# Attention and feed-forward kernel: the hand-written order of the first 16 heads becomes priorities, and the first loads leave on two queues

## The chip, the cores and the metric

The kernel runs on one core of a Trainium2 chip. The metric is device time in microseconds (us) of one execution, as the median of three. The core has five engines with queues of their own: PE (matrix products), DVE (vector), ACT (scalar and activation), POOL, and SP, which here only issues transfers. Each works off its queue in order, so an instruction that waits holds up all behind it on that engine. Transfers between the device's memory and the on-chip memory run on 16 DMA engines; SP and ACT can issue them, and a waiting issue on ACT holds up ACT's arithmetic too.

## What is computed

Eight batches of eight heads of attention, 512 local and 32 global rows, in which a local row sees the 32 global keys and a window of its neighbours, and a global row sees all. The result goes through a feed-forward net with a squared ReLU.

```
s_ll = where(|i - j| <= 32, scale * q_l @ k_l.T, -1e9)
out_l = softmax([scale * q_l @ k_g.T, s_ll]) @ [v_g, v_l]
out_g = softmax(scale * q_g @ [k_g, k_l].T) @ [v_g, v_l]
x = rows of [out_g, out_l], 4608 x 512
h = x @ w_in                      # 512 x 2048, given in float64
g = s * relu(h)**2 + b
out = g @ w_out                   # 2048 x 512, given in float64
```

## The kernel before, in words

A "head" j below is one head for half of the local rows; there are 128, and 16 belong to a batch. For each head PE makes the scores (tile `ps_s`), DVE masks them and takes the least negated value (`least`, tiles `sm`, `nm`), ACT takes exponentials with their sums, DVE the inverses, DVE or ACT divides, PE transposes the result (`turned`), ACT copies it (`pt`) and PE multiplies it by the values (`ps_o`). The scores of the global rows go to `ps_g` and are copied by ACT to `sg`. Eight heads fill one tile of 256 tokens, which is split in a high and a low part (`xst`) for products in three passes.

The feed-forward net takes a tile of tokens in eight groups m: `ps_h` (24 products with w_in), then r = relu on ACT, its square on DVE (`r`), a high part g on ACT, a low part on DVE, and 12 products with w_out into `acc`. Group m of the first tile needs the weight pieces k = 2m and 2m+1. `ps_h` has two buffers: group m+2 can start when `r` of group m is done.

The weights arrive as float64 words, 1 MB for each k (two transfers of 512 KB into `wst`), and are turned into a high and a low float32 part on the chip: `word_exponents` (ACT, L159), `word_shift` (DVE, L165), `word_join` (DVE, L169), `word_high` (a cast on ACT, L174), `word_low` (DVE, L178). There are three staging places, and piece k+3 is loaded when `word_low` of piece k is done. Pieces 0 to 3 go through in two halves each.

The first 16 heads, the 16 weight pieces and the first feed-forward groups make up the "front". Heads 0 to 9 run alone (`head_step`), from head 10 on with a feed-forward group each (`both_step`). In this part the code says in which order ACT, DVE, PE and SP do their work: the loop over j in `window_attention_then_ffn` stands in a `manual_schedule` block, and `behind` keeps some splits of heads 16 to 18 in the written order. After it a scheduler places all instructions by priorities and its own estimate of their durations. POOL and ACT's or DVE's later work is always placed so.

The loads of the first heads are issued by SP (`load32`, `v_load32`, `qg_load`), and the first weight piece by ACT. A transfer may be issued only when the one eight before it in issue order, on whichever queue, has landed, since eight completion counters are used in turn.

At the start PE runs 14 products on constants (`keep_busy`, tile `warm`), then four more after each of the first three heads' scores.

Of the kernel before, what the change touches and what calls it, by code (L numbers as in the profile page):

```python
# [22 lines left out]
P = 128  # L23
# [17 lines left out]


NF = 16
AHEAD = 50


LAG = 10
SPLIT_AT = {8 * t + 9: t for t in range(1, 16)}
# [6 lines left out]
BY_HALVES = 4  # L55
LOADS_AT = {1: 1, 3: 2}
EARLY = 1
KEPT = 19
X_ACT = lambda j: LAG <= j < NF
G_AT = (13, 18)  # L60
G_TR = 3
# [5 lines left out]
def f32(ap):  # L67
    return ap.bitcast(F32)
# [3 lines left out]
def window_attention_then_ffn(ctx: ExitStack, tc: tile.TileContext, qd, qg, kw, vw, vg, qz, qgz, vz, w_in, w_out, sv, bv, out):  # L72
# [67 lines left out]
    def weight_load(k):  # L140
        st = ops.tile([P, 2048], I32, tag=SPOTS[k], name=f"wst{k}", bufs=1 + (SPOTS[k] == "kq"))
        staged[k] = st
        sources = (w_in[k], w_out[k * P:(k + 1) * P, :])
        for i in range(2):
            queue = nc.scalar if k == 0 else nc.sync
            queue.dma_start(st[:, 1024 * i:1024 * (i + 1)], sources[i])
# [57 lines left out]
        nc.sync.dma_start(rv, vw[b, hf, h])  # L204
        st_["rv", j] = rv

    def behind(j, done):
        if j < KEPT:
            tc.keep_in_program_order(done)

    def split(j):
        b, hf, h = slot(j)
        rk, rq = st_.pop(("rk", j)), st_.pop(("rq", j))
        p0 = 64 * (h % 2)
        p1 = 64 - p0
        if h % 2 == 0:
            st_["kq", j] = st_["kq", j + 1] = ops.tile([P, 2048], F32R, tag="kq", name=f"kq{j}", bufs=2)
        kq = st_.pop(("kq", j))[:, 1024 * (h % 2):1024 * (h % 2) + 1024]
        ks, qs = kq[:, 0:NK], kq[:, 512:1024].rearrange("p (i q) -> p i q", i=2)
        behind(j, nc.scalar.copy(out=ks[p0:p0 + 64], in_=rk[p0:p0 + 64]))  # L220
        (nc.gpsimd if K_POOL(j) else nc.vector).tensor_sub(out=ks[p1:p1 + 64], in0=rk[p0:p0 + 64], in1=f32(ks[p0:p0 + 64]))
        behind(j, nc.scalar.copy(out=qs[:, 0, :], in_=rq))  # L222
        nc.gpsimd.tensor_sub(out=qs[:, 1, :], in0=rq, in1=f32(qs[:, 0, :]))  # L223
        st_["ks", j], st_["qs", j] = ks, qs

    def v_split(j):
        rv = st_.pop(("rv", j))
        vs = ops.tile([P, 3, 2, D], F32R, tag="vs", name=f"vs{j}", bufs=2)
        rv4 = rv.rearrange("p (c d) -> p c d", d=D)
        behind(j, nc.scalar.copy(out=vs[:, :, 0, :], in_=rv4))  # L230
        nc.gpsimd.tensor_sub(out=vs[:, :, 1, :], in0=rv4, in1=f32(vs[:, :, 0, :]))  # L231
        st_["vs", j] = vs

# [65 lines left out]
    first_q = ops.tile([P, 1280], F32, tag="vsg", name="first_q", bufs=1)  # L299
    first_v = sb.tile([P, 1280], F32, tag="pg", name="first_v", bufs=1)  # L300

    def load32(j):
        b, hf, h = slot(j)
        if h % 2 == 0:
            if j % 4 == 0:
                rk = sb.tile([P, NK], F32, tag="rk", name=f"rk{j}", bufs=2)
            else:
                rk = ops.tile([P, 384], F32, tag="vs", name=f"rk{j}", bufs=2)[:, 0:NK]
            nc.sync.dma_start(rk, kw[b, hf, h // 2])
            st_["rk", j] = st_["rk", j + 1] = rk  # L310
        rq = first_q[:, HALF * (j % 5):HALF * (j % 5 + 1)]
        nc.sync.dma_start(rq, qz[j])
        st_["rq", j] = rq

    def v_load32(j):
        if j >= NF:
            return
        i = j % 5
        rv = first_v[:, 384 * i:384 * i + 384] if i < 3 else sb.tile([P, 6 * D], F32, tag="rv", name=f"rv{j}")
        nc.sync.dma_start(rv, vz[j])  # L320
        st_["rv", j] = rv

# [58 lines left out]
    def pv32(j):  # L381
        pv_products32(j)
        pv_copy32(j)
# [165 lines left out]
    def g_load(b, h):  # L549
        rv = sb.tile([P, 10 * D], F32, tag="rvg", name=f"rvg{b}_{h}", bufs=1)  # L550
        loaded = nc.sync.dma_start(rv, vg[b, h // 2])
        if b == 0:
            tc.keep_in_program_order(loaded)
        vs = ops.tile([P, 2, 5, 2, D], F32R, tag="vsg", name=f"vsg{b}_{h}", bufs=1)
        for i in range(2):
            rv5 = rv[:, 5 * D * i:5 * D * (i + 1)].rearrange("p (c d) -> p c d", d=D)
            copied = nc.scalar.copy(out=vs[:, i, :, 0, :], in_=rv5)  # L557
            if b == 0:
                tc.keep_in_program_order(copied)
            nc.gpsimd.tensor_sub(out=vs[:, i, :, 1, :], in0=rv5, in1=f32(vs[:, i, :, 0, :]))  # L560
        st_["vsg", b, h] = vs
# [33 lines left out]
    def xg_split(t):
        xs = split_tile(f"xs{t % 2}", f"xst{t}", [2, 4, HALF], 1)
# [190 lines left out]
    def first_steps(j):  # L787
        (head_step if j < LAG else both_step)(j)
# [15 lines left out]
    v_load32(2)
    with tc.manual_schedule(engines={mybir.EngineType.Activation, mybir.EngineType.DVE, mybir.EngineType.PE, mybir.EngineType.SP}):
        scores32(0)
        least(0, st_.pop(("ps", 0)))
        scores32(1)
        for j in range(NF):
            if j == 3:  # L810
                nc.sync.dma_start(s_t, sv.partition_broadcast(P))
                nc.sync.dma_start(b_t, bv.partition_broadcast(P))
            if j in LOADS_AT:
                weight_load(LOADS_AT[j])
            if j == 14:
                qg_load(1)
            first_steps(j)
            for fn in extra.pop(j, []):
                fn()
            if j == NF - 1:  # L820
                ffn_relu(j - LAG)
                ffn_square(j - LAG)
                ffn_high(j - LAG)
                ffn_low(j - LAG)
                turned32(j)
                pv32(j)
                x_split(SPLIT_AT.pop(17))
                split(NF)
                qg_split(1)
# [115 lines left out]
```

## Time and profile before

| | us |
|---|---|
| median of 3 runs | 1018.52 |
| lowest and highest | 1017.27, 1020.16 |
| time of the profiled execution | 1017.95 |
| its span, first to last instruction | 1016.1 |
| PE busy | 990.6 |
| DVE busy | 800.1 |
| ACT busy | 693.9 |

The profiled execution lies 1.85 us around its span. "Busy" of PE counts modelled ends of products that overlap, so it overstates how full PE is where little is to be done. The granted TensorE clock was 1.000, that is, the upper of its two levels.

### The profile page before, as it was taken

How to read it: one execution, taken by the hardware profiler on the slowest of the kernel's cores; microseconds unless marked ns; L12 is line 12 of the kernel's file. 1: busy time of each engine (PE TensorE's matmuls, PEld its weight loads, DVE VectorE, ACT ScalarE, POOL GpSimd, SP SyncE). 2: the span in 40 equal slices, each digit the busy share in tenths (PEclk: the TensorE clock that was granted, in tenths of full speed). 3: DMA queues.
4: the chain of work that ended last, by engine and by line, in shares of the span. 5: the costliest groups of instructions: out<-in, count | busy, mean ns of one | idle time of the engine just before them, and what ended most of it. 6: DMA issues, size and time to landing. Idle time of an engine off the chain costs nothing.

```text
span 1016.1 us, 19944 instructions
## 1 busy us (share of the span) xinstructions
PE 990.6 (97%) x6914; PEld 902.4 (89%) x6914; DVE 800.1 (79%) x2054; ACT 693.9 (68%) x1784; POOL 287.2 (28%) x366
## 2 busy tenths in 40 slices
PE   8798999999999999999999999999999999999998
PEld 5687998989989999999999999999999999999887
DVE  5898778988789788988799788988789788964322
ACT  6998768767677667867678667867678666843222
POOL 1000424424243223424244223424244223401000
PEclk9999999999999999999999999999999999999999
DMA  8873322313132122312132122312132122101000
GB/s 278 304 266 135 95 65 69 91 43 95 31 106 67 49 60 65 91 48 85 45 104 66 44 67 65 91 48 86 44 105 60 49 68 65 61 1 49 23 22 21
DMA packets 63844, 82.03 MB, mean 81 GB/s; under 512 B 7680, under 2 KB 51200, under 8 KB 63744
## 3 DMA queue, kind: packets, MB, share of 16 engines
q1 hardware_dynamic: 63168, 79.46, 25.8%
q10 hardware_dynamic: 576, 1.31, 0.4%
q8 instruction: 54, 0.88, 0.4%
q14 instruction: 46, 0.38, 0.1%
HBM read 71.30 MB, written 9.44 MB: 79 GB/s over the span
## 4 chain that ended last, share of the span: by engine, by line
PE 88%; DVE 5%; ACT 3%; DMA 2%; issue 1%; SPq 0%; DVEq 0%; ACTq 0%
PE acc L664 35%; PE ps_h L620 34%; PE ps_s L441 5%; PE ps_o L469 4%; PE turned L361 2%; PE turned L363 2%; PE ps_og L568 2%; PE ps_g L448 1%; PE turned L542 1%; DMA wst<-in_w_in 1%; PE warm L106 1%; ACT wst L159 1%; DMA wst<-in_w_out 1%; DVE sm L272 1%; DVE sm L242 0%
## 5 line engine op out<-in xcount | busy, mean ns | idle before, releaser
L620 PE MATMUL ps_h<-xst,w_all 128*128 128x256 f32 x3264 | 436.6, 281 | 4.4 <-DVE r L640 1.9
L664 PE MATMUL acc<-w_all,g 128*128 128x512 f32 x1632 | 421.0, 396 | 0.0
L620 PEld LDWEIGHTS ps_h<-xst,w_all 128*128 128x128 f32 x3264 | 408.6, 189 | 12.9 <-DVE r L640 2.1
L664 PEld LDWEIGHTS acc<-w_all,g 128*128 128x128 f32 x1632 | 289.9, 188 | 50.1
L231 POOL TENSOR_TENSOR vs<-rv,vs 128x192 fp32r<-128x192 f32 x112 | 71.4, 638 | 299.9 <-ACT vs L230 287.4
L252 ACT ACTIVATE sm<-sm,nm 128x224 f32<-128x224 f32 x256 | 121.6, 478 | 34.0 <-DVE nm L242 32.9
L640 DVE SCALAR_TENSOR_TENSOR r<-ps_h,s_t,r 128x512 f32<-128x512 f32 x136 | 101.5, 746 | 54.1 <-ACT r L636 52.3
L648 DVE SCALAR_TENSOR_TENSOR g<-r,b_t,g 128x512 fp32r<-128x512 f32 x136 | 110.6, 813 | 39.3 <-ACT g L644 35.2
L644 ACT ACTIVATE g<-r,b_t 128x512 fp32r<-128x512 f32 x136 | 98.5, 725 | 62.1 <-DVE r L640 61.8
L223 POOL TENSOR_TENSOR kq<-rq,kq 128x256 fp32r<-128x256 f32 x112 | 90.0, 804 | 141.6 <-ACT kq L222 129.5
L636 ACT ACTIVATE r<-ps_h 128x512 f32<-128x512 f32 x136 | 81.3, 598 | 69.8 <-PE ps_h L620 61.8
L560 POOL TENSOR_TENSOR vsg<-rvg,vsg 128x320 fp32r<-128x320 f32 x64 | 57.5, 919 | 190.8 <-ACT vsg L557 190.7
L272 DVE TENSOR_SCALAR sm<-sm,nm 128x224 f32<-128x224 f32 x234 | 87.2, 413 | 3.7
L441 PE MATMUL ps_s<-kq 128*128 128x224 f32 x448 | 72.8, 275 | 1.8 <-DVE nm L242 1.8
L441 PEld LDWEIGHTS ps_s<-kq 128*128 128x128 f32 x448 | 66.6, 190 | 8.2 <-POOL kq L223 1.4
L458 ACT CAST pt<-turned 128x416 fp32r<-128x416 f32 x112 | 57.4, 512 | 21.2 <-PE turned L363 20.5
L459 DVE TENSOR_TENSOR pt<-turned,pt 128x416 fp32r<-128x416 f32 x112 | 65.5, 585 | 7.2 <-ACT pt L458 6.5
L452 ACT COPY tg<-ps_g 32x256 f32<-32x256 f32 (+1 forms) x112 | 42.1, 376 | 36.9 <-PE ps_g L448 34.9
L361 PE MATMUL turned<-ident,sm 128*96 128x128 f32 (+1 forms) x256 | 63.3, 273 | 3.8 <-DVE sm L272 2.6
L453 DVE TENSOR_TENSOR sg<-ps_g,tg 32x256 f32<-32x256 f32 (+1 forms) x112 | 48.2, 431 | 21.4 <-ACT tg L452 14.8
L469 PE MATMUL ps_o<-pt,vs 128*128 128x256 f32 x336 | 63.0, 295 | 0.3 <-DVE pt L459 0.3
L363 PE MATMUL turned<-ident,sm 128*128 128x128 f32 x256 | 62.8, 272 | 0.0
(85 smaller groups left out, 1249.7 us busy)
## 6 DMA issues: line engine op xcount, KB each, us to landing
rq<-in_qd SPq DMA_DIRECT2D x112, 128.0 KB, 2.2
rk<-in_kw SPq DMA_DIRECT2D x64, 176.0 KB, 2.3
rv<-in_vw SPq DMA_DIRECT2D x112, 96.0 KB, 1.9
rvg<-in_vg SPq DMA_DIRECT2D x32, 320.0 KB, 3.0
out<-o SPq DMA_DIRECT2D x32, 256.0 KB, 2.3
wst<-in_w_in SPq DMA_DIRECT2D x15, 512.0 KB, 3.9
wst<-in_w_out SPq DMA_DIRECT2D x15, 512.0 KB, 5.4
first_q<-in_qz SPq DMA_DIRECT2D x16, 128.0 KB, 4.9
```

The costliest lines, as they stand in the source:

```text
L223: nc.gpsimd.tensor_sub(out=qs[:, 1, :], in0=rq, in1=f32(qs[:, 0, :]))
L252: nc.scalar.activation(out=p, in_=p, func=AF.Exp, bias=nm[:, 0, blk:blk + 1], scale=-1.0, accum_out=nm[:, 1, blk:blk + 1],)
L272: nc.vector.tensor_scalar(out=p, in0=p, scalar1=ss[:, blk:blk + 1], scalar2=1.0, op0=ALU.mult, op1=ALU.mult,)
L361: nc.tensor.transpose(out=p_t[0:n, s0:s0 + P], in_=sm[:, c0:c0 + n], identity=ident)
L363: nc.tensor.transpose(out=p_t[:, o0:o0 + P], in_=sm[:, c0:c0 + P], identity=ident)
L441: nc.tensor.matmul(p_s[:, W * blk:W * blk + W], lhsT=qs[:, a, blk * P:(blk + 1) * P], rhs=ks[:, KEYS[blk]], start=(a == 0), stop=(a == 1),)
L469: nc.tensor.matmul(p_o[:, :, q], lhsT=vs[0:n, c], rhs=pt[0:n, :, o], start=(c == 0), stop=(c == 1))
L620: nc.tensor.matmul(p_h[:, k], lhsT=wi[:, a, f, c], rhs=xs[:, e, c, :], start=(n == 0), stop=(n == 11),)
L640: nc.vector.scalar_tensor_tensor(out=r, in0=p_h, scalar=s_t, in1=r, op0=ALU.mult, op1=ALU.mult)
L644: nc.scalar.activation(out=g[:, 0], in_=st_["r", m], func=AF.Identity, bias=b_t)
L648: nc.vector.scalar_tensor_tensor(out=g[:, 1], in0=st_.pop(("r", m)), scalar=b_t, in1=f32(g[:, 0]), op0=ALU.add, op1=ALU.subtract,)
L664: nc.tensor.matmul(oacc[t][i], lhsT=g[:, a, k, i * P:(i + 1) * P], rhs=wo[:, e, f, :], start=(pr == 0 and n == 0), stop=(pr == 7 and n == 5),)
```

## The change

The block that fixed the order in the front is gone. The same code in the same sequence now gives priorities, and the scheduler places the instructions on all engines; `behind` and the three other marks that kept program order are gone as well. The loads of the first heads are written in another order and on two queues: the queries of heads 0 and 2, the global queries and the values of head 1 are issued by ACT, the rest by SP, and the first weight piece comes behind the keys and queries of heads 0 to 2 on ACT's queue. The constant AHEAD was not used.

```
-    def load32(j):
+    def load32(j, queue=nc.sync):
...
-        nc.sync.dma_start(rq, qz[j])
+        queue.dma_start(rq, qz[j])
...
-        behind(j, nc.scalar.copy(out=ks[p0:p0 + 64], in_=rk[p0:p0 + 64]))
+        nc.scalar.copy(out=ks[p0:p0 + 64], in_=rk[p0:p0 + 64])
...
     with tc.high_priority(offset=300):
-        load32(0)
+        load32(0, nc.scalar)
         load32(1)
-        qg_load(0)
-        load32(2)
+        qg_load(0, nc.scalar)
+        load32(2, nc.scalar)
         v_load32(0)
+        weight_load(0)
         load32(3)
-        v_load32(1)
-    load32(4)
-    weight_load(0)
-    v_load32(2)
-    with tc.manual_schedule(engines={mybir.EngineType.Activation, mybir.EngineType.DVE, mybir.EngineType.PE, mybir.EngineType.SP}):
-        scores32(0)
-        least(0, st_.pop(("ps", 0)))
-        scores32(1)
-        for j in range(NF):
...
+        v_load32(1, nc.scalar)
+        load32(4)
+        v_load32(2)
+    scores32(0)
+    least(0, st_.pop(("ps", 0)))
+    scores32(1)
+    for j in range(NF):
...
```

What this does to the queues is seen at three places. In the rows the digits behind a name are the head, the group or the piece (`sm1` is head 1, `r4` group 4, `wst13` piece 13), and the last number is the scheduler's own. Lines of the changed kernel are 2 to 9 lower (L174 becomes L172, L640 becomes L632).

ACT at its start, before:

```order
L146 DMA wst0_150<-in_w_in 128x1024
L131 ACT_TABLE_LOAD
L131 ACTIVATE unread_131<-warm_92 128x1
L146 DMA wst0_150<-in_w_out 128x1024
L252 ACTIVATE sm0_165,nm0_166<-sm0_165,nm0_166 128x224 x2
L350 COPY sg0_159<-ps_g1_177 64x256
L270 ACTIVATE sm0_165<-sm0_165,nm0_166 128x224
L252 ACTIVATE sm1_185,nm1_186<-sm1_185,nm1_186 128x224 x2
L377 COPY pt0_224<-turned_83 128x416
L159 ACTIVATE wst0_150<-wst0_150 128x512
L270 ACTIVATE sm1_185<-sm1_185,nm1_186 128x224
L252 ACTIVATE sm2_215,nm2_216<-sm2_215,nm2_216 128x224 x2
```

ACT at its start, now, from its fifth load down to the exponentials of head 2:

```order
L144 DMA wst0_145<-in_w_out 128x1024
L314 DMA first_v_134<-in_vz 128x384
L129 ACT_TABLE_LOAD
...
L157 ACTIVATE wst0_145<-wst0_145 128x512
L344 COPY sg0_157<-ps_g1_175 64x256
L246 ACTIVATE sm0_163,nm0_164<-sm0_163,nm0_164 128x224 x2
L172 CAST w_all_60<-wst0_145 128x512
...
L264 ACTIVATE sm0_163<-sm0_163,nm0_164 128x224
L344 COPY sg0_157<-ps_g3_220 64x256
L246 ACTIVATE sm1_183,nm1_184<-sm1_183,nm1_184 128x224 x2
...
L371 COPY pt0_222<-turned_83 128x416
L246 ACTIVATE sm2_213,nm2_214<-sm2_213,nm2_214 128x224 x2
```

Four loads (queries of head 0, global queries, queries of head 2, the w_in half of piece 0) stand ahead of these rows. Among the rows left out are the exponents of the second half of piece 0 and its cast. So both halves of piece 0 pass through ACT between the first three heads, and the table load has moved behind six loads, of which the fifth and the sixth wait for a landing (the queries of head 0, and the global queries).

DVE at the end of the front, from group 4's square to group 5's, before:

```order
L640 SCALAR_TENSOR_TENSOR r4_934<-ps_h4_867,s_t_90,r4_934 128x512
L258 TENSOR_SCALAR nm15_864<-nm15_864 128x2
L165 TENSOR_SCALAR wst14_851<-wst14_851 128x1024
L262 RECIPROCAL nm15_864<-nm15_864 128x2
L648 SCALAR_TENSOR_TENSOR g4_958<-r4_934,b_t_91,g4_958 128x512
L169 SCALAR_TENSOR_TENSOR wst14_851<-wst14_851 128x1024
L178 TENSOR_TENSOR w_all_60<-wst14_851,w_all_60 128x1024
L165 TENSOR_SCALAR wst15_897<-wst15_897 128x1024
L169 SCALAR_TENSOR_TENSOR wst15_897<-wst15_897 128x1024
L178 TENSOR_TENSOR w_all_60<-wst15_897,w_all_60 128x1024
L640 SCALAR_TENSOR_TENSOR r5_1002<-ps_h5_938,s_t_90,r5_1002 128x512
```

The same stretch now:

```order
L632 SCALAR_TENSOR_TENSOR r4_932<-ps_h4_865,s_t_90,r4_932 128x512
L167 SCALAR_TENSOR_TENSOR wst13_811<-wst13_811 128x1024
...
L176 TENSOR_TENSOR w_all_60<-wst13_811,w_all_60 128x1024
L167 SCALAR_TENSOR_TENSOR wst14_849<-wst14_849 128x1024
L640 SCALAR_TENSOR_TENSOR g4_956<-r4_932,b_t_91,g4_956 128x512
L176 TENSOR_TENSOR w_all_60<-wst14_849,w_all_60 128x1024
L163 TENSOR_SCALAR wst15_895<-wst15_895 128x1024
L167 SCALAR_TENSOR_TENSOR wst15_895<-wst15_895 128x1024
L215 TENSOR_TENSOR kq16_1016<-rk16_675,kq16_1016 64x352
L632 SCALAR_TENSOR_TENSOR r5_1000<-ps_h5_936,s_t_90,r5_1000 128x512
```

The join and the low part of piece 13 have moved from ahead of group 4's square to behind it, the low part of piece 15 behind group 5's, and the split of head 16's keys ahead of that.

PE over the same stretch, before:

```order
L620 MATMUL ps_h5_938<-xst0_294,w_all_60 128x256 x12
L620 MATMUL ps_h6_1065<-xst0_294,w_all_60 128x256 x19
L394 MATMUL ps_o15_953<-pt14_951,rv14_551 128x128 x2
...
L620 MATMUL ps_h5_938<-xst0_294,w_all_60 128x256 x12
...
L664 MATMUL acc0_0_655<-w_all_60,g4_958 128x512 x6
L664 MATMUL acc0_1_656<-w_all_60,g4_958 128x512 x6
L620 MATMUL ps_h6_1065<-xst0_294,w_all_60 128x256 x5
L620 MATMUL ps_h7_1147<-xst0_294,w_all_60 128x256 x24
```

And now:

```order
L612 MATMUL ps_h5_936<-xst0_292,w_all_60 128x256 x16
L612 MATMUL ps_h6_1062<-xst0_292,w_all_60 128x256
L656 MATMUL acc0_0_653<-w_all_60,g4_956 128x512 x2
...
L612 MATMUL ps_h6_1062<-xst0_292,w_all_60 128x256 x15
L388 MATMUL ps_o15_951<-pt14_949,rv14_549 128x128 x2
...
L612 MATMUL ps_h6_1062<-xst0_292,w_all_60 128x256 x8
L435 MATMUL ps_s16_1034<-kq16_1016 128x224
L442 MATMUL ps_g16_1039<-kq16_1016,qgs1_1021 64x256
L435 MATMUL ps_s16_1034<-kq16_1016 128x224 x3
L612 MATMUL ps_h7_1144<-xst0_292,w_all_60 128x256 x8
```

All 24 products of group 5 now stand ahead of group 6's first, which waits for `r4`; 12 of them stood behind it. The scores of head 16 stand ahead of group 7's products, which wait for `r5`.

Names apart, the two orders are the same on PE from its product 2,310 of 6,828 on, and on ACT and DVE from a like place.

## Rows read from the trace of the kernel before

**Rows 1.** Busy time by stretch: from:to, length, engines, PEclk, DMA share, GB/s.
```profile
0.00:20.00 20.00, 17.84 (x80) 10.51 (x80) 8.64 (x37) 10.92 (x31) 3.19 (x15) 1.00 0.81 260
20.00:40.00 20.00, 15.72 (x92) 11.60 (x90) 17.82 (x64) 19.35 (x56) 0.00 (x0) 1.00 0.96 345
40.00:88.00 48.00, 39.85 (x262) 35.04 (x262) 44.39 (x85) 43.21 (x81) 0.00 (x0) 1.00 0.78 266
88.00:300.00 212.00, 206.82 (x1477) 190.76 (x1477) 174.50 (x450) 151.78 (x400) 75.54 (x93) 1.00 0.24 70
300.00:940.00 640.00, 640.00 (x4556) 591.56 (x4555) 532.34 (x1389) 448.52 (x1186) 206.72 (x257) 1.00 0.22 64
```

**Rows 2.** Start of the timeline: start, length, engine, line, operation, idle before and releaser.
```profile
1.19 1.28 ACT L131 ACT_TABLE_LOAD   x1 [1.19 <-PEq L933]
1.46 5.34 PE L106 MATMUL warm<-warm 128*128 128x512 bf16 x14 [1.46 <-DVE warm L101]
5.05 0.33 SPq L320 DMA_DIRECT2D first_v<-in_vz  x1
6.63 0.92 PE L328 MATMUL ps_s<-rk,first_q 128*128 128x224 f32 x4
8.15 0.48 ACT L252 ACTIVATE sm<-sm,nm 128x224 f32<-128x224 f32 x1 [5.46 <-DVE nm L242]
10.98 0.36 ACT L350 COPY sg<-ps_g 64x256 f32<-64x256 f32 x1 [1.79 <-PE ps_g L340]
13.23 0.51 ACT L377 COPY pt<-turned 128x416 f32<-128x416 f32 x1 [0.57 <-PE turned L363]
13.63 0.67 ACT L159 ACTIVATE wst<-wst 128x512 f32<-128x512 f32 x1
...
14.57 0.47 ACT L252 ACTIVATE sm<-sm,nm 128x224 f32<-128x224 f32 x1
15.41 0.19 ACT L252 ACTIVATION_READ_ACCUMULATOR sm<-sm,nm 128x1 f32 x1
```

**Rows 3.** Who waited for whom from 8 to 88 us: total, times, longest.
```profile
ACT w_all L174 <- DVE wst L165: 3.5, 4, 1.2
```

**Rows 4.** Groups by form, front (first three) and 88 to 350 us: busy, mean ns.
```profile
L174 ACT CAST w_all<-wst 128x1024 fp32r<-128x1024 f32 x11 | 12.7, 1157 | 3.5 <-DVE wst L165 3.5
L174 ACT CAST w_all<-wst 128x512 fp32r<-128x512 f32 x8 | 5.4, 670 | 0.0
L169 DVE SCALAR_TENSOR_TENSOR wst<-wst 128x1024 int32<-128x1024 int32 x11 | 13.5, 1223 | 0.1
...
L220 ACT CAST kq<-rk 64x352 fp32r<-64x352 f32 x38 | 18.3, 482 | 0.5
L222 ACT CAST kq<-rq 128x256 fp32r<-128x256 f32 x38 | 15.3, 404 | 1.4 <-DMA rq<-in_qd 1.0
L221 DVE TENSOR_TENSOR kq<-rk,kq 64x352 fp32r<-64x352 f32 x19 | 14.9, 782 | 0.6
```

**Rows 5.** First global queries' transfer (KB, us to landing); weight halves' landing times, all.
```profile
rqg<-in_qgz SPq DMA_DIRECT2D x1, 128.0 KB, 5.2
...
DMA to landing us min/median/max: 3.5/4.6/8.6
```

**Rows 6.** Timeline, scores of head 11 and the end of the front.
```profile
38.46 1.02 PE L328 MATMUL ps_s<-rk,first_q 128*128 128x224 f32 x4
...
86.98 0.74 DVE L640 SCALAR_TENSOR_TENSOR r<-ps_h,s_t,r 128x512 f32<-128x512 f32 x1
87.78 2.45 PE L620 MATMUL ps_h<-xst,w_all 128*128 128x256 f32 x19 [1.88 <-DVE r L640]
93.45 0.63 ACT L636 ACTIVATE r<-ps_h 128x512 f32<-128x512 f32 x1
94.86 0.75 DVE L640 SCALAR_TENSOR_TENSOR r<-ps_h,s_t,r 128x512 f32<-128x512 f32 x1
95.39 3.58 PE L620 MATMUL ps_h<-xst,w_all 128*128 128x256 f32 x29
```

More of the change, by code (lines that the diff above doesn't have):

```diff
@@ L43 @@
 NF = 16
-AHEAD = 50
 LAG = 10
@@ L57 @@
 EARLY = 1
-KEPT = 19
 X_ACT = lambda j: LAG <= j < NF
@@ L205, in v_load @@
         st_["rv", j] = rv
-    def behind(j, done):
-        if j < KEPT:
-            tc.keep_in_program_order(done)
     def split(j):
@@ L219, in split @@
         ks, qs = kq[:, 0:NK], kq[:, 512:1024].rearrange("p (i q) -> p i q", i=2)
-        behind(j, nc.scalar.copy(out=ks[p0:p0 + 64], in_=rk[p0:p0 + 64]))
+        nc.scalar.copy(out=ks[p0:p0 + 64], in_=rk[p0:p0 + 64])
         (nc.gpsimd if K_POOL(j) else nc.vector).tensor_sub(out=ks[p1:p1 + 64], in0=rk[p0:p0 + 64], in1=f32(ks[p0:p0 + 64]))
-        behind(j, nc.scalar.copy(out=qs[:, 0, :], in_=rq))
+        nc.scalar.copy(out=qs[:, 0, :], in_=rq)
         nc.gpsimd.tensor_sub(out=qs[:, 1, :], in0=rq, in1=f32(qs[:, 0, :]))
@@ L229, in v_split @@
         rv4 = rv.rearrange("p (c d) -> p c d", d=D)
-        behind(j, nc.scalar.copy(out=vs[:, :, 0, :], in_=rv4))
+        nc.scalar.copy(out=vs[:, :, 0, :], in_=rv4)
         nc.gpsimd.tensor_sub(out=vs[:, :, 1, :], in0=rv4, in1=f32(vs[:, :, 0, :]))
@@ L311, in load32, with v_load32 @@
         rq = first_q[:, HALF * (j % 5):HALF * (j % 5 + 1)]
-        nc.sync.dma_start(rq, qz[j])
+        queue.dma_start(rq, qz[j])
         st_["rq", j] = rq
-    def v_load32(j):
+    def v_load32(j, queue=nc.sync):
         if j >= NF:
@@ L319, in v_load32 @@
         rv = first_v[:, 384 * i:384 * i + 384] if i < 3 else sb.tile([P, 6 * D], F32, tag="rv", name=f"rv{j}")
-        nc.sync.dma_start(rv, vz[j])
+        queue.dma_start(rv, vz[j])
         st_["rv", j] = rv
@@ L415, in pv_copy32, with qg_load @@
             nc.vector.tensor_copy(out=x_out, in_=p_o)
-    def qg_load(b):
+    def qg_load(b, queue=nc.sync):
         rqg = sb.tile([P, H * SG], F32, tag="xr", name=f"rqg{b}", bufs=1)
-        nc.sync.dma_start(rqg, qgz[0] if b == 0 else qg[b])
+        queue.dma_start(rqg, qgz[0] if b == 0 else qg[b])
         st_["rqg", b] = rqg
@@ L551, in g_load @@
         loaded = nc.sync.dma_start(rv, vg[b, h // 2])
-        if b == 0:
-            tc.keep_in_program_order(loaded)
         vs = ops.tile([P, 2, 5, 2, D], F32R, tag="vsg", name=f"vsg{b}_{h}", bufs=1)
@@ L587, in x_split @@
                 v = slice(2 * i, 2 * i + 2)
-                behind(8 * t + 8, nc.scalar.copy(out=xs_[t][:, 0, v, :], in_=xcur[t][:, v, :]))
+                nc.scalar.copy(out=xs_[t][:, 0, v, :], in_=xcur[t][:, v, :])
         if only != 0:
@@ L592, in x_split @@
                 v = slice(2 * i, 2 * i + 2)
-                behind(8 * t + 8, nc.vector.tensor_sub(out=xs[:, 1, v, :], in0=x[:, v, :], in1=f32(xs[:, 0, v, :])))
+                nc.vector.tensor_sub(out=xs[:, 1, v, :], in0=x[:, v, :], in1=f32(xs[:, 0, v, :]))
     def xg_split(t):
@@ L794, in window_attention_then_ffn @@
     with tc.high_priority(offset=300):
-        load32(0)
+        load32(0, nc.scalar)
         load32(1)
-        qg_load(0)
-        load32(2)
+        qg_load(0, nc.scalar)
+        load32(2, nc.scalar)
         v_load32(0)
+        weight_load(0)
         load32(3)
-        v_load32(1)
-    load32(4)
-    weight_load(0)
-    v_load32(2)
-    with tc.manual_schedule(engines={mybir.EngineType.Activation, mybir.EngineType.DVE, mybir.EngineType.PE, mybir.EngineType.SP}):
-        scores32(0)
-        least(0, st_.pop(("ps", 0)))
-        scores32(1)
-        for j in range(NF):
[L810 to L829, printed above, removed]
+        v_load32(1, nc.scalar)
[5 more added lines that the diff above has]
+    for j in range(NF):
+        if j == 3:
+            nc.sync.dma_start(s_t, sv.partition_broadcast(P))
+            nc.sync.dma_start(b_t, bv.partition_broadcast(P))
+        if j in LOADS_AT:
+            weight_load(LOADS_AT[j])
+        if j == 14:
+            qg_load(1)
+        first_steps(j)
+        for fn in extra.pop(j, []):
+            fn()
+        if j == NF - 1:
+            ffn_relu(j - LAG)
+            ffn_square(j - LAG)
+            ffn_high(j - LAG)
+            ffn_low(j - LAG)
+            turned32(j)
+            pv32(j)
+            x_split(SPLIT_AT.pop(17))
+            split(NF)
+            qg_split(1)
     assert not to_join and not staged and not g_at
```

## The prediction

> **What bounds the kernel now.** I read busy time by stretch first. From 88 us on PE is full: 206.8 of 212 us, then 640 of 640 [rows 1]. From about a third of PE's work on, the two orders are the same, so the change can alter the time in two ways only: by how early PE becomes full, and by the 5.2 us that it stands still between 88 and 300 us. A microsecond saved in the front is then one saved at the end.
>
> In the front PE is not the limit. From 20 to 40 us ACT works 19.35 of 20 us and the transfers take 0.96 of the DMA engines; from 40 to 88 us DVE works 44.4 and ACT 43.2 of 48 us [rows 1]. What may be gained there is the idle time of these two, some 4 us each, and what the start leaves. The timeline shows the start: ACT has nothing to do until 8.15 us, waits 1.79 us more before 10.98, and touches the first weights only at 13.63 [rows 2]. Later ACT's longest wait is that of its cast of the high part, 3.5 us in four cases, for DVE's shift, the instruction just ahead in the same chain [rows 3]. Last I read the end of the front: PE's products of group 6 stand 1.88 us for `r` of group 4 until 87.78; group 7's follow at 95.97 (95.39 and five products of 0.12 us), right behind `r` of group 5, which ends at 95.61 [rows 6]. There PE catches up with ACT and DVE for the last time.
>
> **The change part by part.** *Keys and queries earlier, on two queues.* The first scores follow the 14 warm-up products without a gap (1.46 and 5.34 give 6.80; the first scores' record begins at 6.63) [rows 2], and these products stay. So earlier keys are worth nothing at the first head. Without that cover they would be worth at most one landing, 5.2 us for a load of this size [rows 5].
>
> The Trainium skill, in "DMA: Bandwidth & Descriptors", section "Issuing engines are not separate DMA queues", says that the transfers of all issuers share the same 16 DMA engines and that a second issuer saves only issue time. By it the three loads of queries that leave SP would give at most 1.2 us, at 0.4 us each; by the warm-up's row it is 0. The trace agrees in so far as almost all loads from 20 to 40 us are SP's, and they take 0.96 of the engines.
>
> The price lies on ACT. It has six issues ahead of its table load, and the fifth and sixth wait for landings of the first loads. In the old run the ninth transfer, which waits for the first one's landing, left at 5.05 us [rows 2]; the global queries took 5.2 us to land [rows 5], so after an issue at 1.2 they would let the sixth go at 6.4. With issues of 0.3 to 0.4, the table load of 1.28 [rows 2] and a small activation of 0.2 us, ACT is free between 6.9 and 8.4 us. I take 7.4. The exponents of the first half (0.67) and the copy of global scores (0.36) then put the first exponentials at 8.4 rather than 8.15 [rows 2].
>
> *The first three heads.* From 8.4 the new order has on ACT: exponentials of heads 0, 1 and 2, each a pair with its sum reads, 1.03 us a head (14.57 to 15.60 [rows 2]); two casts of 0.67 [rows 4]; the second exponents of 0.67, one division of 0.47, taken as an exponential's, a copy of 0.36 and a `pt` copy of 0.51 [rows 2]. That is 6.4 us, so head 2's exponentials could be done at 14.8. Before they are done at 15.60 (15.41 and 0.19). At that point the new order has two casts, one half of exponents and one copy more behind it and one division less: 1.34 + 0.67 + 0.36 - 0.47 = 1.9 us. The lead is 0.8 + 1.9 = 2.7 us if nothing waits, 1.7 if ACT is free only at 8.4. DVE has the join and the low part of the same halves between the heads, and PE's next scores wait for DVE, so I take 2.0.
>
> *Heads 3 to 10.* ACT has 0.65 us of idle time left in 20 us and the DMA engines 0.04 of theirs [rows 1], so nothing is gained here, and a lead can be lost. Summed along the issue order, the new one has 10.7 MB out by the keys of heads 14 and 15, among them 0.59 MB that the old one left for later (queries of heads 16 and 17, global values). It wants these keys, for `ps_g15`, ahead of the scores of head 11, which began at 38.46 [rows 6]. The old run had moved 5.2 MB by 20 and 12.1 MB by 40 us; at 345 GB/s it stood at 10.7 MB at 35.9 [rows 1]. The margin is 2.6 us, a little more than the lead, so I keep the lead.
>
> *Heads 10 to 15.* The new order puts other work between a shift and its cast. Of the 3.5 us of these waits [rows 3] I take 1.0 as gained, between 0 (DVE is 92% busy, so ACT then waits elsewhere) and 2.4 us. With the start this is R = 3.0 us, between 1.7 and 5.1.
>
> *The end of the front.* For `r` of group 4 DVE has a join and a low part less ahead (1.22 us each [rows 4]), so group 6 can start 2.4 us earlier and R on top, with 12 products more behind it. But most of this is given back. Ahead of `r` of group 5 ACT has one cast less (1.16) and more: two casts of keys (0.48) and two of queries (0.40) [rows 4], one of global queries and one of values (about 0.4 each, taken as the queries'), net 1.4 us. Its `r` ended at 94.08 and DVE took it at 94.86 [rows 6]; now ACT ends at 94.08 + 1.4 - 3.0 = 92.5. DVE has a low part less and a split of keys more (1.22 against 0.78 [rows 4]), so it is free at 91.4, and `r` is done at 93.2. Group 7 thus starts 2.8 us earlier than 95.97, and PE has the four score products of head 16 behind it, 0.6 us at five times a 0.12 us product. PE gains 3.4 us. Between the two gates it stands still for some 3.5 us: the old stretch of 8.2 us, less 12 products, plus these scores, is 7.4, and the gates lie 11 us apart. For group 8 ACT's splits add 5.3 us, of which R takes 3.0; the other 2.3 lie beside group 7's 24 products (2.8 us) and the output products behind them.
>
> *From 88 to 350 us.* The scheduler placed this part before and does so now, from another state. The 5.2 us of waits [rows 1] may shrink or grow; I take no change, and 2 us either way.
>
> *The other edits.* Where the unmarked splits went is counted above. The constant AHEAD costs nothing, since no instruction used it.
>
> The sum: 1017.95 for the profiled execution, less 3.4, is 1014.5. That execution lies 0.6 us under the median of the three runs, so I say **1014.8 us**, between the two.
>
> **The rivals.** *No net gain.* The front is a reshuffle: ACT and DVE are 90 to 97% busy, and what the start gains is waited out at their next crossing. For it: the idle time from 20 to 88 us is made of waits of about 1 us or less [rows 3]. Against it: the idle time at the start is of another kind, for there was nothing to do. R is then 1.0, group 7 gains 0.8 us, and the time is 1017.5 by the median.
>
> *A larger gain.* R is 5.1 and the later waits halve: 1017.95 - 5.5 - 2.6, about 1010. For it: DVE is what PE waits for at the end, and it loses 2.4 us of work ahead of that place. Against it: two engines over 90% busy and in order rarely pack closer.
>
> *Late keys, slower.* The place is `ps_g15` on PE, ahead of head 11's scores: PE's queue stands until the keys of heads 14 and 15 land, and ACT and DVE have at most one head in stock. SP issues these keys behind two half loads of weights that wait for DVE. Weight halves took 4.6 us to land in the median and 8.6 at most [rows 5]; keys 4.0 us late use up the margin of 2.6, and earlier loads pass the same stretch. If the lead is lost and 3.6 us with it, the time is 1021.6. It decides when these keys land after 38.5 us. For it: 0.96 of the DMA engines busy, and 0.59 MB (1.7 us at 345 GB/s) brought forward into that stretch. Against it: from 40 to 88 us the share is only 0.78 [rows 1], so the queue recovers.
>
> **How the numbers follow.** A difference under 0.3% (3.1 us) is about what a measurement of this kernel can't tell from none. I give 0.40 to the forecast, with its own range of 1013 to 1016.5, of which 0.30 lies below 1015.4; 0.15 to the larger gain; 0.25 to no net gain; 0.20 to late keys. So faster is 0.45 (0.30 and 0.15), same 0.35 (0.10 and 0.25), and slower 0.20. The range goes from 1009.5, just under the larger gain's time, to 1021.0; beyond it lie most of late keys and a few hundredths below.
>
> **What would show it.** On ACT the first exponents at 7 to 8 us, the first exponentials at 8.3 to 9, and head 2's done before 15.3. PE's group 6 starting at 82 to 84 us, group 7 at 92 to 94 behind a wait for `r` of about 3 us, and no wait at `ps_g15`. ACT's waits for the shift well under 3.5 us. PE full from group 7 on, with 3 to 7 us of waits up to 350 us. The forecast fails if PE waits for a load between 20 and 40 us, if group 7 starts later than 95, or if the waits behind it grow by more than 3 us.

## The result, and the profile after

The changed kernel takes **1005.92 us** (1004.15 to 1006.82) against 1019.34 for the kernel before: a ratio of 0.9867, with a 95% interval of 0.9841 to 0.9893. That is 13.4 us faster; the prediction had 1014.8, with a range from 1009.5 to 1021.0, so the result lies 3.6 us below its lower end. The direction was right and the size was not. The profiled execution took 1005.12 us, its span 1003.3. The ratios, here and below, leave out three executions that took far longer than the others of their kernel (1992.87 us of E2, 1098.31 of E5 and 1227.64 of the kernel before).

Busy time by stretch in the changed kernel, with the columns and stretches of [rows 1]:

```profile
0.00:20.00 20.00, 17.57 (x76) 9.69 (x77) 11.25 (x42) 12.68 (x35) 3.19 (x15) 1.00 0.79 272
20.00:40.00 20.00, 16.02 (x94) 12.37 (x92) 18.36 (x65) 19.89 (x55) 0.00 (x0) 1.00 1.04 389
40.00:88.00 48.00, 46.13 (x311) 43.13 (x310) 45.07 (x88) 45.76 (x89) 3.20 (x3) 0.96 0.72 243
88.00:300.00 212.00, 211.44 (x1513) 195.31 (x1512) 182.14 (x475) 155.51 (x414) 80.42 (x95) 1.00 0.26 74
300.00:940.00 640.00, 640.00 (x4562) 591.81 (x4561) 526.18 (x1364) 443.21 (x1168) 204.72 (x254) 1.00 0.22 62
```

Two things are to be seen. PE's idle time before 88 us (length less the first busy number) fell from 14.6 to 8.3 us, most of it between 40 and 88 us: 1.9 us against 8.2. And from 88 to 300 us it fell from 5.2 to 0.6. Together that is 10.9 us. PE's busy time over the whole span fell by 1.7 (990.6 to 988.9), so 12.6 of the span's 12.8 us are accounted for. From 300 to 940 us PE is full in both.

The same view in finer steps shows from when on PE is full:

```profile
40.00:46.00 6.00, 4.13 (x29) 3.52 (x28) 5.58 (x16) 5.95 (x13) 0.00 (x0) 1.00 1.01 379
46.00:50.00 4.00, 4.00 (x21) 4.00 (x22) 3.72 (x10) 4.00 (x8) 0.00 (x0) 0.57 0.86 287
50.00:88.00 38.00, 38.00 (x264) 35.61 (x263) 35.78 (x64) 35.81 (x70) 3.20 (x3) 1.00 0.66 217
```

It is full from 46 us, not from 88. Four rows of its timeline and the two squares `r` that the prediction spoke of show how:

```profile
21.29 0.96 PE L612 MATMUL ps_h<-xst,w_all 128*128 128x256 f32 x3
...
78.32 0.74 DVE L632 SCALAR_TENSOR_TENSOR r<-ps_h,s_t,r 128x512 f32<-128x512 f32 x1
81.25 2.12 PE L612 MATMUL ps_h<-xst,w_all 128*128 128x256 f32 x17
...
89.45 0.75 DVE L632 SCALAR_TENSOR_TENSOR r<-ps_h,s_t,r 128x512 f32<-128x512 f32 x1
...
90.76 0.59 PE L435 MATMUL ps_s<-kq 128*128 128x224 f32 x3 [0.56 <-POOL kq L217]
91.19 1.10 PE L612 MATMUL ps_h<-xst,w_all 128*128 128x256 f32 x8
```

The first feed-forward products run at 21.29 us, in ones to fours between the heads, where the old order had them in blocks of twelve from 41.81 on. The square of group 4 ends at 79.06, that of group 5 at 90.20, 8.7 and 5.4 us earlier than in [rows 6]. PE waits for neither: the last of the 17 products at 81.25 is group 6's first, 4 us after its gate opened, and group 7 follows at 91.19. PE's one wait between 88 and 300 us is the 0.56 us before 90.76, for the split of head 16's keys on POOL.

ACT's waits from 8 to 88 us (the view of [rows 3]) have changed their kind:

```profile
ACT wst L157 <- DMA wst<-in_w_in: 2.4, 1, 2.4
ACT wst L157 <- DMA wst<-in_w_out: 1.6, 3, 0.9
ACT r L628 <- PE ps_h L612: 0.6, 1, 0.6
```

The 3.5 us behind DVE's shift are gone whole; what is left are mostly waits for weights to land.

### The profile page after: what moved, and what is told of

The parts are those of the page before. It is cut to its first block, busy times and chain, and to the rows that moved or that the text cites. A ratio compares the mean times of both kernels' runs of the same rounds, so it can differ in the third digit from the quotient of the medians.

```text
span 1003.3 us, 19931 instructions
## 1 busy us (share of the span) xinstructions
PE 988.9 (99%) x6914; PEld 903.6 (90%) x6914; DVE 800.9 (80%) x2054; ACT 693.5 (69%) x1784; POOL 291.5 (29%) x366
## 4 chain that ended last, share of the span: by engine, by line
PE 90%; DMA 4%; ACT 3%; DVE 1%; issue 1%; SPq 0%; POOL 0%; ACTq 0%; POOLq 0%
PE acc L656 36%; PE ps_h L612 36%; PE ps_s L435 5%; PE ps_o L463 4%; PE turned L355 2%; PE turned L357 2%; PE ps_og L560 2%; DMA wst<-in_w_out 2%; PE ps_g L442 1%; PE turned L536 1%; DMA rk<-in_kw 1%; ACT wst L157 1%; ACT w_all L172 1%; DMA first_q<-in_qz 1%; DMA b_t<-in_bv 1%
## 5 line engine op out<-in xcount | busy, mean ns | idle before, releaser
L632 DVE SCALAR_TENSOR_TENSOR r<-ps_h,s_t,r 128x512 f32<-128x512 f32 x136 | 101.5, 746 | 54.6 <-ACT r L628 52.7
L640 DVE SCALAR_TENSOR_TENSOR g<-r,b_t,g 128x512 fp32r<-128x512 f32 x136 | 111.7, 822 | 36.0 <-ACT g L636 31.6
L217 POOL TENSOR_TENSOR kq<-rq,kq 128x256 fp32r<-128x256 f32 x112 | 93.1, 832 | 138.2 <-ACT kq L216 122.2
L266 DVE TENSOR_SCALAR sm<-sm,nm 128x224 f32<-128x224 f32 x234 | 84.3, 400 | 4.1
```

The source lines that it names most:

```text
L266: nc.vector.tensor_scalar(out=p, in0=p, scalar1=ss[:, blk:blk + 1], scalar2=1.0, op0=ALU.mult, op1=ALU.mult,)
L640: nc.vector.scalar_tensor_tensor(out=g[:, 1], in0=st_.pop(("r", m)), scalar=b_t, in1=f32(g[:, 0]), op0=ALU.add, op1=ALU.subtract,)
```

## Experiments

The theory after the result (A): the gain has two separate causes. ACT, DVE and PE pack closer in the first 100 us, and the attention of the later heads runs ahead of the feed-forward groups when the weights are done, so that PE no longer waits for it between 100 and 300 us. Rivals are named in each expectation. All results stand in one table. "Idle" is the length of the stretch less PE's busy time; "lead" is how long before DVE's square of group 9 the first exponential of head 18 starts on ACT; "clock" is the mean granted clock of the span. Each ratio is taken against the kernel before on the same chip at the same time. Idle time, lead and clock are those of one execution of each kernel.

| kernel | median us | ratio (95%) | idle 0-100 | idle 100-300 | lead | clock |
|---|---|---|---|---|---|---|
| before | 1018.1 to 1019.7 | 1 | 14.6 | 5.2 | 1.1 | 1.000 |
| the change | 1005.9 | 0.9867 (0.9841-0.9893) | 8.8 | 0.0 | 8.2 | 0.998 |
| E1 loads alone | 1019.5 | 1.0007 (0.9996-1.0017) | 14.5 | 5.4 | 1.1 | 0.998 |
| E2 free order alone | 1003.6 | 0.9853 (0.9838-0.9867) | 7.9 | 0.8 | 8.0 | 1.000 |
| E3 marks off | 1019.2 | 1.0009 (0.9997-1.0021) | 12.6 | 3.6 | -0.1 | 0.991 |
| E4 free from head 10 | 1015.3 | 0.9962 (0.9947-0.9976) | 8.7 | 3.2 | 6.4 | 0.995 |
| E5 free to head 9 | 1020.3 | 1.0013 (1.0001-1.0025) | 13.4 | 3.5 | 2.4 | 0.991 |
| E6 ACT, DVE free | 1009.7 | 0.9922 (0.9908-0.9935) | 11.8 | 0.5 | 8.0 | 0.998 |
| E7 PE, SP free | 1023.0 | 1.0055 (1.0036-1.0074) | 14.3 | 6.3 | -0.1 | 0.994 |
| E8 heads 18, 19 late | 1019.4 | 1.0015 (1.0006-1.0024) | 8.4 | 9.8 | -13.1 | 0.992 |
| E9 weights first | 1013.1 | 0.9945 (0.9931-0.9958) | 10.2 | 4.1 | 2.4 | 0.996 |
| E10 one queue | 1003.6 | 0.9851 (0.9838-0.9865) | 8.2 | 0.5 | 8.0 | 1.000 |
| E11 heads to 31 early | 1004.4 | 0.9854 (0.9841-0.9868) | 8.6 | 0.0 | 7.3 | 1.000 |
| E12 heads 18, 19 less late | 1011.0 | 0.9920 (0.9906-0.9933) | 8.3 | 4.9 | 0.2 | 0.998 |
| E13 written, lag 12 | 1025.6 | 1.0061 (1.0047-1.0075) | 23.0 | 0.0 | 15.5 | 0.990 |
| E14 free, lag 12 | 1012.2 | 0.9928 (0.9912-0.9945) | 8.1 | 1.8 | 5.4 | 0.999 |

**E1 and E2: the two halves of the change.** E1 is the kernel before with the new loads, E2 the changed kernel with the old ones.

```
     with tc.high_priority(offset=300):
-        load32(0)
+        load32(0, nc.scalar)
         load32(1)
-        qg_load(0)
-        load32(2)
+        qg_load(0, nc.scalar)
+        load32(2, nc.scalar)
         v_load32(0)
+        weight_load(0)
...
```

> The written order and its marks stay; only the first loads are issued in the new order and on two queues. Theory A: the gain of 13 us has two causes, both from the free order: PE stands idle 8.3 us before 88 us instead of 14.6, and its waits of 5.2 us between 150 and 300 us are gone. The loads give next to nothing, since the warm-up products cover them: 1017 to 1020 us, 3 to 6 us of PE waits between 88 and 300 us. Rival B: earlier keys, queries and values give the head start that all the rest inherits: 1008 to 1013 us.

> The scheduler places the first 16 heads, and the first loads leave in the old order, nearly all on SP. Theory A: nearly the whole gain, 1005 to 1009 us, with PE idle about 8 us before 88 us and under 1 us of PE waits from 88 to 300 us. Rival B: most of the gain is lost with the loads, 1013 to 1018 us.

Busy time from 0 to 100 and 100 to 300 us, of E1:

```profile
0.00:100.00 100.00, 85.55 (x505) 68.33 (x506) 79.64 (x195) 80.73 (x176) 3.19 (x15) 0.98 0.72 250
100.00:300.00 200.00, 194.64 (x1386) 179.11 (x1386) 163.59 (x435) 142.75 (x385) 74.92 (x92) 1.00 0.24 73
```

and of E2:

```profile
0.00:100.00 100.00, 92.12 (x573) 76.68 (x574) 88.11 (x213) 89.70 (x204) 16.09 (x26) 1.00 0.75 264
100.00:300.00 200.00, 199.22 (x1426) 183.87 (x1425) 169.95 (x458) 145.85 (x391) 70.75 (x87) 1.00 0.24 71
```

Theory B falls. E2 is even 1.4 us faster than theory A allowed, though its waits from 88 to 300 us are 2.3 us and not under 1. The loads are worth nothing in the written order, and the free order has the whole gain without them: all three engines do 7 to 9 us more work in the first 100 us than in E1. E2's span is 1.6 us below the changed kernel's at the same idle time (8.7 against 8.8 us); the difference is in PE's busy time (987.3 against 988.9), and the changed kernel has the stretch from 46 to 50 us at a granted clock of 0.57, E2 none below 1.00 before its end.

**E3, E6 and E7: which engines must be free.** Old loads, no marks; the block stands around the same code with all four engines (E3), PE and SP (E6), or ACT and DVE (E7).

```
...
-    for j in range(NF):
...
+    with tc.manual_schedule(engines={mybir.EngineType.PE, mybir.EngineType.SP}):
...
+        for j in range(NF):
...
```

> The written order of the first 16 heads stays and the loads leave as before; only the marks that keep splits of heads 16 to 18, the splits of the first tiles and the first global values in the written order are gone. Theory A: the front is unchanged and the attention of heads 16 to 19 stays late (exponentials of head 16 at about 109 us), so the PE waits from 150 to 300 us stay: 1016 to 1020 us, 4 to 6 us of waits from 88 to 300 us. Rival D: it is the marks that held the later attention back; without them those waits go: 1011 to 1015 us.

> Old loads, no marks; PE and SP keep the written order for the first 16 heads, ACT and DVE are placed by the scheduler. Theory A: before 88 us ACT and DVE are over 90% busy and PE only follows, so their free order gives most of the gain: 1005 to 1010 us, PE idle 8 to 10 us before 88 us. Rival E: what gains is PE's free order, which puts feed-forward products into PE's waits, gets the squares of the groups out earlier and so the heads of the free placement: 1013 to 1019 us, PE idle 12 to 15 us.

> Old loads, no marks; ACT and DVE keep the written order for the first 16 heads, PE and SP are placed by the scheduler. Theory A: ACT and DVE hold all else to their pace: 1014 to 1019 us, the square of group 4 at 85 to 88 us. Rival E: PE's free order carries the gain: 1005 to 1011 us, the square of group 4 under 82 us.

The same two stretches, of E6:

```profile
0.00:100.00 100.00, 88.23 (x530) 70.70 (x531) 82.73 (x201) 86.03 (x193) 12.47 (x24) 0.98 0.75 258
100.00:300.00 200.00, 199.46 (x1425) 184.08 (x1424) 169.79 (x449) 144.78 (x387) 69.88 (x87) 1.00 0.24 72
```

and of E7:

```profile
0.00:100.00 100.00, 85.71 (x488) 68.42 (x488) 77.28 (x191) 79.62 (x176) 6.56 (x19) 0.95 0.73 253
100.00:300.00 200.00, 193.69 (x1377) 178.24 (x1378) 164.51 (x429) 140.78 (x376) 69.49 (x85) 1.00 0.22 66
```

With E2 this is a square: 1019.2 us with all written, 1009.7 with ACT and DVE free, 1023.0 with PE and SP free, 1003.6 with all free. ACT's and DVE's freedom carries the gain, and PE's is worth 6 us on top of it but costs 4 without it. In E6 the larger part of the gain is the second cause: the waits from 100 to 300 us are gone, while PE is idle 11.8 us before 100, where theory A had expected 8 to 10 before 88. So E6 has A's time, and an idle time just under what rival E had said. E7 is 4 us slower than A allowed, and its square of group 4 starts at 91.38 us, where A had 85 to 88. The marks alone do nothing for the time, and rival D falls. E3 also shows that idle time is not the whole account: PE waits 3.6 us less up to 300 us than in the kernel before, but is busy for 7.5 us longer (998.1 against 990.6) at a clock of 0.991.

**E4 and E5: which part of the front.** Loads as changed; the written order for heads 0 to 9 alone (E4) or for heads 10 to 15 alone (E5).

```
...
-    for j in range(NF):
+    MAN = dict(engines={mybir.EngineType.Activation, mybir.EngineType.DVE, mybir.EngineType.PE, mybir.EngineType.SP})
+    with tc.manual_schedule(**MAN):
...
+        for j in range(LAG):
...
+    for j in range(LAG, NF):
...
```

> Loads as changed; the written order is kept for heads 0 to 9 and the scheduler places from head 10 on. Theory A: the gain of the first 88 us is won where PE catches up with ACT and DVE, at heads 10 to 15, and the later waits go as well: 1006 to 1011 us. Rival C: the gain is made in heads 0 to 9, where the free order gets the weights some 6 us earlier through ACT and DVE and starts the first feed-forward products at 21 instead of 42 us: 1014 to 1018 us.

> Loads as changed; the scheduler places heads 0 to 9, and the written order holds for heads 10 to 15. Theory A: little of the gain before 88 us is left, and the later waits come back as far as they hang on heads 10 to 15: 1012 to 1017 us. Rival C: most of the gain before 88 us stays, 6 to 7 us: 1007 to 1012 us.

Theory A misses both times. E4's time lies in rival C's range, but E5 speaks against C's reason: heads 0 to 9 alone bring nothing, where C had 1007 to 1012 us. Neither half has much of the gain: 0.4% and none. E4 wins the first cause (idle 8.7 us) but keeps 3.2 us of the later waits at a clock of 0.995; E5 keeps most of the idle time (16.9 of 19.8 us up to 300 us). The freedom has to reach over the whole front.

**E8, E12 and E11: the lead of the attention.** E2 with another priority for the heads behind the front: lower for heads 16 to 19 (an offset of -300 in E8 and -100 in E12, where E2 has +50), higher for heads 16 to 31 (+300, E11). The front stays: idle 8.3 to 8.6 us before 100 us against 7.9.

```
             if NF <= j < 20:
-                with tc.high_priority(offset=50):
+                with tc.high_priority(offset=-300):
```

> Free placement with the loads as before (the version that took 1003.6 us); only heads 16 to 19 get a lower priority, so that the scores and exponentials of heads 18 and 19 stand behind group 9 instead of ahead of it. The front up to about 95 us stays. Theory A: PE's waits between 150 and 300 us were gone because the attention runs ahead of the feed-forward net from head 16 on; they come back, 3 to 6 us: 1006 to 1010 us. Rival F: those waits depend on how the scheduler packs each stretch, not on this lead: 1002 to 1005 us, with under 2.5 us of waits.

> As the version in which the lower priority of heads 16 to 19 cost 15.8 us, with a third of the shift: the exponentials of heads 18 and 19 stand 9 and 5 rows later on ACT than in the free placement, there 17 and 15. Theory A: the price follows the lead that is lost, 1006 to 1013 us, with 2 to 8 us of PE waits from 88 to 300 us. Rival F: no such order, so about as dear as the large shift or free of cost: over 1015 or under 1005 us.

> Free placement with the old loads (1003.6 us, 2.3 us of PE waits between 88 and 300 us); heads 16 to 31 instead of 16 to 19 get a higher priority, which moves exponentials by a few places from head 19 on. Theory A: the more the attention runs ahead, the fewer PE waits are left: 1001 to 1003 us. Rival F: the rest of the waits is a matter of how single stretches are packed: 1003 to 1006 us.

In the changed kernel head 18's first exponential and group 9's square run at these times:

```profile
105.57 0.49 ACT L246 ACTIVATE sm<-sm,nm 128x224 f32<-128x224 f32 x1
...
113.80 0.74 DVE L632 SCALAR_TENSOR_TENSOR r<-ps_h,s_t,r 128x512 f32<-128x512 f32 x1
```

and in E8 at these:

```profile
112.17 0.73 DVE L632 SCALAR_TENSOR_TENSOR r<-ps_h,s_t,r 128x512 f32<-128x512 f32 x1
...
125.22 0.48 ACT L246 ACTIVATE sm<-sm,nm 128x224 f32<-128x224 f32 x1
```

PE's waits from 100 to 300 us in E8 (total, times, longest):

```profile
PE ps_o L463 <- POOL kq L217: 3.7, 1, 3.7
PE ps_g L442 <- DVE sg L447: 3.0, 4, 1.8
PE ps_o L463 <- DVE pt L453: 1.5, 2, 1.1
PE ps_s L435 <- DVE kq L215: 1.2, 1, 1.2
PE turned L536 <- DVE pt L453: 0.4, 1, 0.4
```

and in E12:

```profile
PE ps_s L435 <- DVE nm L236: 2.1, 2, 1.5
PE ps_h L612 <- DVE xst L585: 1.6, 1, 1.6
PE ps_g L442 <- DVE sg L447: 0.9, 1, 0.9
PE ps_o L463 <- DVE pt L453: 0.3, 1, 0.3
```

All are waits for the attention's chain, `xst` being the split of its result. So were those of the kernel before from 100 to 300 us:

```profile
PE ps_s L441 <- DVE nm L242: 1.8, 2, 1.2
PE ps_h L620 <- DVE xst L593: 1.6, 1, 1.6
PE ps_g L448 <- DVE sg L453: 1.4, 1, 1.4
PE ps_o L469 <- DVE pt L459: 0.3, 1, 0.3
```

With the lead cut from 8.0 to 0.2 and -13.1 us, 0.8 us of idle time become 4.9 and 9.8, and the time goes from 1003.6 to 1011.0 and 1019.4: the second cause is shown, and with a good front the lost lead eats the whole gain. It is shown by taking the lead away; no run gives it to the kernel before without moving the feed-forward groups. Over all kernels of the table the later waits fall with the lead, if not strictly: 3.5 to 9.8 us with leads under 3 us, 0 to 0.8 with 7 us and more, E4 and E14 between. E12 came out as theory A had it (1006 to 1013 us); E8 is dearer than expected because PE also runs slower (busy for 995.5 us against E2's 987.3); this is its busy time from 150 to 200 us, where it stood 7.1 us and the granted clock was 0.86:

```profile
150.00:200.00 50.00, 42.87 (x270) 38.63 (x269) 40.43 (x111) 33.62 (x94) 18.09 (x23) 0.86 0.26 77
```

E11 lies in rival F's range and not in A's: its last waits went (0.0 us), with no gain in time that the measurement can tell. It did not give head 18 more lead (7.3 us), so what a longer lead behind an equal front would bring was not tried.

**E9 and E10: the new loads in the free order.** The changed kernel with the first weight piece ahead of the keys (E9), or with all of the heads' loads on SP (E10).

```
+        weight_load(0)
         load32(0, nc.scalar)
         load32(1)
         qg_load(0, nc.scalar)
         load32(2, nc.scalar)
         v_load32(0)
-        weight_load(0)
```

> Free placement, two queues as changed, but the first weight piece is issued ahead of the keys and queries again. The changed kernel took 1005.9 us, the free placement with old loads 1003.6; in the changed one ACT touches the first weights at 8.71 us, behind 2.42 us of waiting. Theory G: the 2 us between the two are the late first weights: 1002.5 to 1004.5 us here. Rival H: they come from ACT's issues, of which two wait for landings ahead of its table load: 1005 to 1007 us here, since these issues stay.

> Free placement and the loads written in the changed order, but all of the first heads' loads on SP and the first weight piece alone on ACT. Theory G (late first weights cost 2 us): ACT has the weights' two halves at once, 1002.5 to 1004.5 us. Rival H (issues on ACT cost them): the same time, 1002.5 to 1004.5 us; a time of 1005 to 1007 us would speak for neither and leave the written order of the loads itself.

E10 is as fast as E2, so the new loads are not needed: these two, at 1003.6 us, are the fastest versions, 2 us under the changed kernel, a difference that the intervals do not quite separate. E10's two theories gave the same time, so it does not decide between them. E9 meets neither of its own: it is 7 us slower than the changed kernel. Its start on ACT:

```profile
6.79 0.34 ACTq L314 DMA_DIRECT2D first_v<-in_vz  x1
7.15 1.28 ACT L129 ACT_TABLE_LOAD   x1 [7.15 <-DMA wst<-in_w_out]
...
11.33 0.48 ACT L246 ACTIVATE sm<-sm,nm 128x224 f32<-128x224 f32 x1
```

The sixth issue leaves only at 6.79, behind the landing of the weights, so H's mechanism is at work here and stronger. Both halves of the first piece then pass through ACT first, and head 0's first exponential starts 1.8 us later than in the changed kernel. The scheduler then places the heads later as well (head 15 at 87.1 against 78.0 us), the lead is 2.4 us, and 4.1 us of waits are back. How much of this the late start does, and how much the other placement, no run here separates.

**E13 and E14: more lead by the constant.** Head j beside group j - 12 instead of j - 10, in the kernel before and in E2.

```
-LAG = 10
+LAG = 12
```

> The kernel before with one constant changed: head j runs beside group j - 12 instead of j - 10, in the front and behind it. The written order stays. Theory A (the time follows the attention's lead): the exponentials of head 18 come some 8 to 12 us earlier than 117.9 us, the PE waits of 150 to 300 us go, and what PE loses in the front by the later start of the feed-forward net counts little: 1006 to 1014 us. Rival I (PE's idle time before 88 us counts in full): the groups start two heads later, PE is idle 5 to 10 us more in the front: 1019 to 1026 us.

> The free placement with the old loads (1003.6 us) and the same constant. Theory A: the lead is already enough there (2.3 us of PE waits are left), so at most these are won: 1001 to 1004 us. Rival I: later groups in the front cost PE time: 1005 to 1010 us.

In E13 the later waits are gone, and yet it is the slowest kernel:

```profile
0.00:100.00 100.00, 76.97 (x423) 59.75 (x424) 76.64 (x193) 76.49 (x167) 3.19 (x15) 0.90 0.72 250
100.00:300.00 200.00, 200.00 (x1431) 185.00 (x1431) 163.50 (x439) 144.75 (x387) 71.74 (x90) 1.00 0.24 68
```

Head 18 did not come earlier (121.1 us); the groups came later, which makes a lead too, but is paid with 8.4 us more of idle time in the front. Rival I's time came true with A's waits: the two causes are separate and both count. E14 lies above both of its ranges. Its idle time up to 300 us is 1.2 us above E2's and its time 8.6; PE's busy time is 6.4 us longer (993.7 against 987.3) for as many products at a clock of 0.999. The constant holds for all heads, and a part of this comes late: from 300 to 940 us, with PE full, 4,545 products against E2's 4,565. Why is open.

## Why the prediction was wrong, step by step

**What the change acts through** was right: the orders are alike later on, and from 300 to 940 us PE is full before and now. That PE is full from 88 us on is true of the kernel before only.

**Keys and queries earlier: 0.** Right: E1's ratio is 1.0007. The Trainium skill ("DMA: Bandwidth & Descriptors", section "Issuing engines are not separate DMA queues") says that issuing transfers from several engines saves only the time of the issue. The trace agrees: E1 moved 250 GB/s in the first 100 us, as the kernel before did. The price on ACT was mis-sized: ACT was free at 6.3 us, before the 7.4 taken, and then waited 2.42 us for the first weights to land, which the sum had not looked for. So the first exponentials came at 9.53 us and not at 8.4. The changed kernel's start on ACT, for [rows 2]:

```profile
4.78 1.28 ACT L129 ACT_TABLE_LOAD   x1 [4.78 <-DMA rqg<-in_qgz]
6.08 0.20 ACT L129 ACTIVATE unread<-warm 128x1 f32<-128x1 bf16 x1
8.71 0.67 ACT L157 ACTIVATE wst<-wst 128x512 f32<-128x512 f32 x1 [2.42 <-DMA wst<-in_w_in]
9.28 0.35 ACT L344 COPY sg<-ps_g 64x256 f32<-64x256 f32 x1
9.53 0.48 ACT L246 ACTIVATE sm<-sm,nm 128x224 f32<-128x224 f32 x1
```

**The first three heads: 2.0.** About right. Head 2's sums ended at 15.40 (15.3 was said), with two casts more behind it, and by 20 us ACT had done 1.8 us more (12.68 against 10.92), the low end of the 1.7 to 2.7 worked out.

**Heads 3 to 10: nothing.** A little low: 0.5 us on either engine between 20 and 40 us. The reason given was partly wrong: the transfers were not at their limit at 0.96 of the engines and 345 GB/s, for they now move 389. PE waited for a load there once, 0.74 us at the global scores that go with head 9:

```profile
23.00 0.70 PE L334 MATMUL ps_g<-rk,rqg 128*64 128x288 f32 x2 [0.74 <-DMA rk<-in_kw]
```

A wait for a load in this stretch was one of the prediction's signs of failure, but 0.74 us are too few to have decided anything, and no wait came at `ps_g15`.

**Heads 10 to 15: 1.0.** Too small. All 3.5 us of waits behind the shift went, and ACT does 2.55 us more from 40 to 88 us, just over the upper bound of 2.4. So R was 4.8 us by ACT's busy time (78.3 against 73.5 before 88 us), 3.8 by DVE's, where 3.0 was taken and 5.1 was the bound.

**The end of the front: 3.4.** This step failed in its mechanism. It took PE for a follower that is let go at two gates and waits between them. The gates opened at 79.06 and 90.20, even before the times that were worked out (82 to 84 and 93.2), but PE reached them late and busy. Group 6 did start inside the 82 to 84 us that were forecast (its first product at about 83.2), but by luck, not because its gate opened then, and the forecast wait of about 3 us behind `r` of group 5 did not come. The old rows had already shown what this missed: PE had 8.2 us of idle time between 40 and 88 us [rows 1], and the new order puts feed-forward products into it. PE's gain before 100 us is 5.8 us where the sum had 3.4. E6 and E7 show that neither PE nor ACT and DVE would have had it alone.

**From 88 to 350 us: no change, 2 us either way.** This step failed too, and is the larger error of reason: of 5.2 us of waits 0.6 were left. The new order had shown the scores of head 16 ahead of group 7's products, and the prediction counted them as 0.6 us of PE's work and nothing else. What stood behind it was the attention's lead (1.1 us before, 8.2 now), and E8 and E12 show that the waits hang on it.

**The rivals.** "A larger gain" was right in kind, R near its bound and fewer later waits, but it halved the waits, and at 1010 was still 4 us short. "No net gain" rested on the engines being too full to pack closer; ACT and DVE went from 82.2 and 80.4 to 89.0 and 86.2 us of work in the first 100. (Its time by its own terms is 1017.7, 1018.52 less 0.8, and not 1017.5.)

## What to carry to other kernels

When an order is freed, sum the idle time of the engine that will be full later, not only the busy time ahead of its last two gates: small products that can start early turn the other engines' waits into its work. Look at the state at the end of a ramp-up as well as at its time: which of two interleaved chains is ahead there decided 5 us (and with E8 all of the gain) over the next 200. An order written for all engines holds together: freeing PE alone was a loss (E7), the first half of the stretch alone brought nothing (E5) and the second half 0.4% (E4).

## What the runs showed of the hardware

The granted clock fell to its lower level (1.2 of 2.4 GHz) in single stretches of 11 of the 16 kernels, each behind waits of PE: in the changed kernel from 46 to 50 us (mean 0.57), after PE stood 1.9 of 6 us; in E8 from 150 to 200 us (0.86, 7.1 us of idle time). But in the kernel before PE stood 4.3 us between 20 and 40 us at 1.00 [rows 1]. And the same wait in the same written order went both ways: behind `r` of group 4 PE stood 1.88 us in the kernel before and 1.81 in E1, and from 90 to 92 us the clock was 1.00 in the one and 0.50 in the other. What makes the clock fall was not tried by itself. What a stretch costs can be read where PE is full: six products with the values took 0.88 us at the upper level, and in the changed kernel at 46.95 us 1.59. The busy share of the transfers' engines is no hard bound: from 20 to 40 us it read 0.96 at 345 GB/s before and 1.04 at 389 after.
